# Two units' MLP by blocks as the weights come, not three; the third and fourth unit's by block products

## The chip, the cores and the metric

The kernel runs on 1 core of one Trainium2 chip. The metric is the device time of one execution in microseconds (us). The core has TensorE (PE; PEld is its weight loads), VectorE (DVE), ScalarE (ACT), GpSimd (POOL) and SyncE (SP), which issues nearly all DMAs here. Each engine works through its own list of instructions in order and waits on semaphores for the others.

## The reference

An outer-product recurrence (HGRN2) for 4 batches, 8 heads, 768 tokens and head dimension 48, and then an MLP without bias over its output, all in f32:

```python
f = 1.0 / (1.0 + np.exp(-f_logit))
for t in range(S):
    state = f[:, :, t, :, None] * state + np.einsum('bhd,bhe->bhde', k[:, :, t], v[:, :, t])
    y[:, :, t] = np.einsum('bhd,bhde->bhe', q[:, :, t], state)
x = np.ascontiguousarray(y.transpose(0, 2, 1, 3)).reshape(B * S, H * D)   # 3072 x 384
h = x @ w_in                                                              # 384 x 2048
g = h * (1.0 / (1.0 + np.exp(-1.702 * h)))
out = g @ w_out                                                           # 2048 x 384
```

## The kernel before, in words

**Units.** The 3072 tokens are cut into 12 units of 256 (`U`), three to a batch. `attention(n)` returns the parts of one unit's recurrence: loads of f, q, k into `raw`, transposes into `F` and `X`, level after level of products of scores (`sc`), the states (`st`) and the output `y`, which ScalarE copies into `yT` and DMAs bring into `xT`, transposed as the MLP wants it. VectorE multiplies X by decays (L519, L523), moves scores into `A` (L466, L485) and computes the states (L667, L668).

**Weights.** w_in and w_out come in 16 pairs of column or row blocks. `fetch_weights` loads a pair into one of three `bits` buffers, and `begin_pair` and `convert` turn it into usable f32: one ScalarE activation (L228) and four VectorE instructions (L230 to L233), the last of which writes `w_in` or `w_out`. The 16 pairs make four blocks of the hidden dimension, each with two pairs of w_in and then two of w_out; pairs 12 and 13 are the fourth block of w_in, 14 and 15 that of w_out. The temporaries are `a` and `s`; `s` has one buffer.

**MLP.** There are three forms. *By blocks* (`mlp_block`, with `mlp_h`, L1100, and `mlp_o`, L1114): per block of four tiles of the hidden dimension, 12 matmuls of 256 columns make h, and 8 of 384 columns make a partial sum of the output, which ScalarE copies to `sum` for the first block and VectorE adds to it for the later ones (L1164, L1166). *h by block products* (`mlp_h20`, L1006): a 4 x 3 by 3 x 2 block product with 20 multiplications of sums of blocks in place of 24, so 80 matmuls of 128 columns in place of 48 of 256. It needs sums of the blocks of x (`E`, twelve additions on GpSimd, `sums_of_x`, L968) and sums of blocks of w_in: nine new tiles `N_c1` to `N_p16` (`sums_of_w`; L930 and L928, mostly on GpSimd), and nine that overwrite w_in itself (`sums_in_place`, four on GpSimd, five on VectorE), after which no plain h is possible. ScalarE and VectorE combine the products into `g` (L1013 to L1036). *o by seven products* (`mlp_o7`, L869): a 2 x 2 block product with seven multiplications, 56 matmuls of 192 columns in place of 32 of 384. It needs sums of quarters of w_out (`T`, `sums_of_b`, L783) and of g (`S`, `sums_of_a`, L804 to L813), on VectorE.

**Who uses which.** Before the change units 0, 1 and 2 go by blocks for both h and o, since the weights are still coming; unit 3 (`mlp_unit`) has plain h and o by seven products, and from unit 4 on both are block products. `N_FILL` is 3.

**Order.** The order of TensorE and GpSimd is written out. `merge(n, fill, columns, share, pieces, ...)` emits the parts of attention unit n in turn, the beginnings of unit n + 1 among them, and after each part so many items of `fill` (the list of MLP matmuls with their columns) as make up its share of `columns`; `pieces` says how many pairs are converted within it and `chores` lists sums to be done in between. Up to `fill_order.close()`, after the merge of unit 3, the order of the other engines is also that of emission; later it is planned by the framework. `LAG`, `UNIT`, `H20` are numbers of columns.

**Banks.** PSUM tiles of the MLP take four banks in turn (`bank`, tags mm0 to mm3); h20 also uses the tags `y` and `sc` of the attention (its lanes 4 and 5 are the tile `h_y`). A product that takes a bank waits for whoever last reads it.

Of the kernel before, what the change touches and what calls it, by code (L numbers as in the profile page):

```python
# [23 lines left out]
def kernel(  # L24
# [33 lines left out]
    nc = tc.nc  # L58
    B, H, S, D = q.shape
    DM = H * D  # L60
# [4 lines left out]
    U = 256  # L65
# [7 lines left out]
    NK = DM // P  # L73
    NFF = DFF // P
    FG = 4
    PAIRS_AHEAD = 3
    N_FILL = 3
    HALF = U // 2
    SLOT = NP * HALF
    NA = NP * U  # L80
# [20 lines left out]
    turns = count()  # L101
# [72 lines left out]
    NGR = NFF // FG  # L174
# [144 lines left out]
    def attention(n):  # L319
# [265 lines left out]
        def turn_k(a0):  # L585
            if a0 == 0:
                new_kn()
            if n < N_FILL + 1:
                pt = bank([P, 2, 2, P], f"tkn_{n}_{a0}")
            else:  # L590
                pt = ps.tile([P, 2, 2, P], F32, tag="sc", name=f"tkn_{n}_{a0}")
            for a in range(2):
                for f in range(2):
                    x = (a0 + a) * HALF
                    nc.tensor.transpose(pt[:, a, f, :], slot((KR, KF)[f])[:, x:x + HALF], ident)
            nc.scalar.copy(t["kn"][:, a0:a0 + 2], pt)
# [75 lines left out]
        def _():  # L672
# [4 lines left out]
            for cs in ((1, 0), (2, 3)):  # L677
                for a in range(NP):
                    for c in cs:
                        g, f = CHUNK[c]  # L680
# [5 lines left out]
                        for h in range(2):  # L686
                            state = t["before"][c][rows(h), a] if w > 1 else t["ahead"][rows(h), NC - 1, a]
                            x = a * HALF + g * HS
# [29 lines left out]
            xTs[n] = xT  # L718
            if n == 0:
                fetch_weights()  # L720
            if n > N_FILL:
                sums_of_x(n)

        def whole(py):
# [402 lines left out]
    def mlp_unit(n, fill):  # L1127
        g, before = {}, []

        def last_token():  # L1130
            po = ps.tile([P, DM], F32, tag="sc", name="o_last")
            nc.tensor.matmul(po[:1], lhsT=ones, rhs=g["last"][:, 0], start=True, stop=True)
            nc.scalar.copy(g["last"][:1, 0], po[:1])
            nc.sync.dma_start(out=out[NALL * U - 1:, :], in_=g["last"][:1, 0])
        o = mlp_o7(n, g)
        if width(n) > U:
            o.insert(6 * HF, (DM, last_token, 0))
        if width(n) > U:
            before = fill[-2 * HF:]
            del fill[-2 * HF:]  # L1140
        if n > N_FILL:
            return mlp_h20(n, g, before) + o
        by_block = {}

        def end():

            g[0], g[1] = (by_block["tile", i] for i in range(2))
            sums_of_a(n, g)
            sums_in_place(nc.gpsimd)
            lanes["o"] = [next(turns) % 4 for _ in range(4)]  # L1150
        return mlp_h(n, range(NFF), by_block) + [(0, end, 0)] + o[:HF] + [(0, lambda: sums_in_place(nc.vector), 0)] + o[HF:]

    sums = {}

# [16 lines left out]
    def mlp_blocks(*blocks):  # L1171

        hs, os = zip(*(mlp_block(n, r) for n, r in blocks))
        return sum(hs, []) + sum(os, [])
# [44 lines left out]
    def merge(n, fill, columns, share, pieces=0, hold=0, by=1.0, chores=[], per=3, deal=()):  # L1219
# [10 lines left out]
        for kind, fn in parts:  # L1230
            ready = state["done"]
            while kind in ("S", "S1") and any(in_y.get(m) for m in range(n)):
                w, emit, _ = fill.pop(0)
                emit()
                done += w
            fn()
            at += share(kind)
            at_ops += converting.get(kind, 0)
            most = pieces * NOP // 2
            n_ops = min(int(most * at_ops / (by * total_ops)), most) - ops  # L1240
            if deal:
                n_ops, deal = deal[0], deal[1:]
            ops += n_ops
            first, n_columns = done, max(0, columns * (at - held) / (total - held) - done)

            def some(end):
                nonlocal done
                while fill and done < end and fill[0][2] <= ready:
                    w, emit, _ = fill.pop(0)
                    emit()  # L1250
                    done += w
            jobs = [convert] * n_ops + chores[:per]
            del chores[:per]
            for i, job in enumerate(jobs):
                some(first + n_columns * i / len(jobs))
                job()
            some(first + n_columns)
# [12 lines left out]
    def opening():  # L1270
# [44 lines left out]
        for _ in range(NOP):  # L1315
            convert()

    fill = []
    opening()
    fill += mlp_blocks((0, 0)) + mlp_blocks((0, 1))  # L1320
    merge(1, fill, UNIT // 2 - LAG // 2 - 3 * DM, steady, 13, hold=1)
    fill += mlp_blocks((1, 0), (1, 1)) + mlp_blocks((0, 2), (1, 2))
    merge(2, fill, UNIT + 3 * DM, steady, 12)
    fill += mlp_blocks((2, 0), (2, 1)) + mlp_blocks((2, 2), (0, 3)) + mlp_blocks((1, 3), (2, 3))
    w_sums = [*sums_of_w(("c3", "p15", "c2", "p6"))]
    merge(3, fill, 3 * UNIT // 2 - LAG // 2, steady, 5, by=0.7, chores=w_sums, per=1)
    fill_order.close()
    for n in range(N_FILL, NALL):
        fill += mlp_unit(n, fill)
    with nc.allow_non_contiguous_dma("one token"):  # L1330
        for h in range(2):
            nc.sync.dma_start(out=q_end[h * HS:h * HS + D], in_=q[B - 1, h::2, S - 1, :].rearrange("a d -> d a"))
    assert not w_sums
    of_b = [*sums_of_b()]
    for x in sums_of_w(("c1", "c4", "p12", "p4", "p16")):
        w_sums += of_b[:1] + [x]
        del of_b[:1]
    w_sums += of_b
    for n in range(4, NALL):
        merge(n, fill, (H20 if n > N_FILL + 1 else NFF * NK * U) + 7 * HF * HC, late, chores=w_sums if n == 4 else [])  # L1340
    for _, emit, _ in fill:
        emit()

# [28 lines left out]
```

## Time and profile before

| | |
|---|---|
| median of 3 runs | 598.24 us (596.16 to 599.87) |
| span of the profiled execution, first to last instruction | 594.5 us |
| TensorE busy, matmuls | 574.9 us, 97% |
| VectorE busy | 429.5 us, 72% |
| ScalarE busy | 291.9 us, 49% |
| GpSimd busy | 138.4 us, 23% |
| plain h, L1100 | 384 passes |
| plain o, L1114 | 192 passes |
| conversions of pairs end (last write of w_out) | 171.7 us from the start |
| first block product of o (unit 3) | 224.0 us |
| first block product of h (unit 4) | 248.4 us |

The span is that of one profiled execution; the runs' time also holds what lies around the first and last instruction, so 594.5 stands beside 598.24, a difference of 3.7 us. A matmul in f32 shows as two passes in the trace, and counts of passes are twice those of the program. In the timeline's rows the columns are start, duration, engine, line, operation, tiles, shape and count, and in brackets the idle time before and who ended it; in the windows' rows they are busy time of PE, PEld, DVE, ACT and POOL, each with its number of instructions, then the granted TensorE clock, the share of DMA and GB/s.

### The profile page before, as it was taken

The page shows a single profiled execution, that of the slowest core. Times are in us where ns is not written, and L with a number is a line of the kernel's source. Part 1 is how long each engine was busy: PE and PEld are TensorE (multiplying, and loading weights), DVE is VectorE, ACT ScalarE, POOL GpSimd, SP SyncE. Part 2 cuts the span into 40 slices and gives each one's busy share as a digit, 9 for nine tenths or more (in the row PEclk, how much of TensorE's full clock was granted, in tenths as well). Part 3 has the DMA queues.
Part 4 walks back from the last instruction along what each step waited for, and adds up shares of the span by engine and source line. Part 5 has one row for each costly group of instructions (what it writes and reads, how often), then busy time and mean ns, then how long its engine had stood idle before and what let it go on. Part 6 is the DMA issues. An engine that isn't in the chain of part 4 may idle for free.

```text
span 594.5 us, 18457 instructions
## 1 busy us (share of the span) xinstructions
PE 574.9 (97%) x7814; PEld 513.6 (86%) x7814; DVE 429.5 (72%) x696; ACT 291.9 (49%) x613; POOL 138.4 (23%) x214
## 2 busy tenths in 40 slices
PE   6879899999999999999999999999999999999997
PEld 6756776867768789999999999999999999999897
DVE  2898987964866858789778778786887786462284
ACT  4746643453334353474474474573663564452440
POOL 4031200230027216610610700800700602203000
PEclk9979999999999999999999999999999999999999
DMA  7947859840243552353552343553361211001000
GB/s 181 215 124 179 193 145 225 217 100 1 52 106 66 145 130 65 80 139 77 127 146 51 84 113 91 130 134 60 88 168 44 63 38 29 28 3 27 28 1 27
DMA packets 82834, 58.29 MB, mean 98 GB/s; under 512 B 33153, under 2 KB 74785, under 8 KB 82753
## 3 DMA queue, kind: packets, MB, share of 16 engines
q1 hardware_dynamic: 82416, 56.73, 38.9%
q8 instruction: 61, 1.00, 0.7%
q10 hardware_dynamic: 337, 0.39, 0.3%
q14 instruction: 20, 0.16, 0.1%
HBM read 43.98 MB, written 8.39 MB: 88 GB/s over the span
## 4 chain that ended last, share of the span: by engine, by line
PE 87%; DVE 7%; ACT 3%; issue 1%; DMA 1%; POOL 1%; SPq 0%; DVEq 0%; ACTq 0%
PE h L1006 17%; PE h L1100 13%; PE o_Y L869 11%; PE o L1114 10%; PE o_Z L869 8%; PE h_y L1006 6%; PE sc L425 6%; PE o_X L869 4%; PE o_W L869 4%; PE y L689 2%; PE t L357 2%; PE y L534 2%; PE sc L643 1%; DVE X L519 1%; ACT yT L703 1%
## 5 line engine op out<-in xcount | busy, mean ns | idle before, releaser
L1100 PE MATMUL h<-xT,w_in 128*128 128x256 f32 x384 | 89.6, 388 | 1.4 <-DMA xT<-yT 1.4
L523 DVE TENSOR_TENSOR X<-X,tot 128x1024 f32<-128x1024 f32 x45 | 57.0, 1266 | 39.8 <-PE sc L425 33.2
L1100 PEld LDWEIGHTS h<-xT,w_in 128*128 128x128 f32 x384 | 72.8, 193 | 13.8 <-DMA xT<-yT 2.4
L494 ACT COPY Kc<-X 128x512 f32<-128x512 f32 x72 | 48.4, 672 | 65.7 <-DVE X L523 51.5
L1114 PE MATMUL o<-w_out,g 128*128 128x384 f32 x192 | 65.5, 491 | 0.4 <-DVE w_out L233 0.4
L968 POOL TENSOR_TENSOR E<-xT 128x128 f32<-128x128 f32 (+1 forms) x32 | 17.9, 571 | 204.0 <-DMA xT<-yT 112.0
L1114 PEld LDWEIGHTS o<-w_out,g 128*128 128x128 f32 x192 | 35.4, 190 | 22.8 <-DVE w_out L233 1.0
L1006 PE MATMUL h<-E,w_in 128*128 128x128 f32 (+1 forms) x420 | 53.4, 275 | 0.0
L869 PE MATMUL o_Y<-T,S 128*128 128x192 f32 x288 | 50.6, 329 | 0.0
L1006 PEld LDWEIGHTS h<-E,w_in 128*128 128x128 f32 x420 | 50.1, 192 | 0.0
L1036 ACT ACTIVATE g<-g 128x512 f32<-128x512 f32 (+1 forms) x63 | 35.6, 584 | 26.0 <-DVE g L1034 25.3
L1104 ACT ACTIVATE g<-h 128x256 f32<-128x256 f32 x64 | 23.8, 382 | 49.0 <-PE h L1100 48.6
L869 PEld LDWEIGHTS o_Y<-T,S 128*128 128x128 f32 x288 | 46.8, 190 | 0.5
L1034 DVE TENSOR_TENSOR g<-g,h 128x512 f32<-128x512 f32 (+1 forms) x52 | 31.8, 632 | 14.3 <-PE h L1006 13.3
L485 DVE COPY_PREDICATED A<-masks,sc 128x256 f32<-128x256 uint32 (+1 forms) x98 | 42.0, 506 | 0.1
L703 ACT COPY yT<-y 48x256 f32<-48x256 f32 x88 | 32.2, 366 | 18.3 <-PE y L689 17.2
L372 POOL TENSOR_SCALAR F<-F 128x1024 f32<-128x1024 f32 x10 | 17.2, 1716 | 95.9 <-ACT F L375 84.3
L345 DVE STREAM_TRANSPOSE X<-raw 128x512 f32<-128x512 f32 x36 | 38.1, 1105 | 0.1
L425 PEld LDWEIGHTS sc<-X,Kc 48*64 48x64 f32 x1440 | 26.2, 136 | 11.1 <-ACT Kc L494 4.8
L425 PE MATMUL sc<-X,Kc 48*64 48x64 f32 x1440 | 31.0, 222 | 4.8 <-ACT Kc L494 1.9
L1034 DVE TENSOR_TENSOR g<-g,h_y 128x512 f32<-128x512 f32 (+1 forms) x26 | 16.5, 634 | 22.3 <-PE h_y L1006 21.4
L1025 ACT ACTIVATE g<-h 128x512 f32<-128x512 f32 (+1 forms) x46 | 26.1, 576 | 10.8 <-PE h L1006 10.6
(162 smaller groups left out, 1156.2 us busy)
## 6 DMA issues: line engine op xcount, KB each, us to landing
bits<-in_moe_w_out_dram SPq DMA_DIRECT2D x8, 768.0 KB, 7.2
raw<-in_f_logit_dram SPq DMA_DIRECT2D x48, 96.0 KB, 3.5
raw<-in_k_dram SPq DMA_DIRECT2D x48, 96.0 KB, 3.0
bits<-in_moe_w_in_dram SPq DMA_DIRECT2D x8, 576.0 KB
raw<-in_q_dram SPq DMA_DIRECT2D x44, 96.0 KB, 2.3
k_tok<-z SPq DMA_DIRECT2D x56, 64.0 KB, 1.8
kt<-k_tok SPq DMA_DIRECT2D x14, 256.0 KB, 2.8
out_dram<-osb SPq DMA_DIRECT2D x18, 192.0 KB, 2.7
```

Of the source, the lines that this page charges most:

```text
L345: nc.vector.transpose(view(out, at, [[HALF, NP], [step, R4], [R4 * step, 32]]), by_half[:, j, f].rearrange("p a (j d) -> p (a j) d", j=R4) ...
L425: nc.tensor.matmul(t["sc"][h][g * HS:(g + 1) * HS, a, s, :], lhsT=t["Kc", l][rows(h), x:x + HS], rhs=rhs(h, a, g), start=True, stop=True,)
L485: moved = nc.vector.copy_predicated(out=view(A, c * HALF + at, dims), mask=mask.bitcast(U32), data=got)
L494: nc.scalar.copy(c.rearrange("p (n two m) -> p n two m", two=2, m=m), view(X, KF * SLOT, [[2 * m, SLOT // (2 * m)], [(KR - KF) * SLOT + m, ...
L523: nc.vector.tensor_tensor(x, x, y, ALU.mult)
L703: nc.scalar.copy(view(yT[rows(h)], at, [[U, NP], [step, HS]]), py[columns(h, g), g, :, f, :])
L869: nc.tensor.matmul(t[name], lhsT=lhs(f), rhs=rhs(f), start=(new and i == 0), stop=(i == HF - 1), skip_group_check=True,)
L1006: nc.tensor.matmul(ph[:, t], lhsT=WA[a][:, f * P:(f + 1) * P], rhs=E[n][b], start=(root and t == 0), stop=not goes_on, skip_group_check=True,)
L1034: nc.vector.tensor_tensor(to, to, part, ALU.add if sign > 0 else ALU.subtract)
L1036: nc.scalar.activation(to, to, AF.Gelu_apprx_sigmoid)
L1100: nc.tensor.matmul(ph, lhsT=w_in[:, c, ff * P:(ff + 1) * P], rhs=xTs[n][:, c, :], start=(c == 0), stop=(c == NK - 1))
L1114: nc.tensor.matmul(t["po"], lhsT=g[ff // FG][:, ff % FG, tt * P:(tt + 1) * P], rhs=w_out[:, ff, :], start=(ff == ffs[0]), stop=(ff == ffs[ ...
```

## The change

`N_BLOCK` is 2: only units 0 and 1 have all four blocks of the plain form. Their fourth block comes from `last_blocks()`, which puts the sums of w_in that are still to be done, the sums of unit 2's x and the sums in place into the list behind the first o of that block. Unit 2 gets h and o by block products (`first_whole`, with the sums of w_out's quarters spread over its h), and unit 3's h becomes block products as well, since `mlp_unit` knows no plain form any more. All nine sums of w_in are chores of the merge of unit 3, two per part, and the last conversions come earlier: 13 pieces in the merge of unit 2 (12 before), 4 in that of unit 3 (5 before), spread over its first part (`by` 0.3, was 0.7). In the later merges every unit has `H20 + 7 * HF * HC` columns and no chores.

```diff
+    N_BLOCK = 2
...
-            if n < N_FILL + 1:
+            if n < N_FILL:
                 pt = bank([P, 2, 2, P], f"tkn_{n}_{a0}")
...
-            if n > N_FILL:
+            if n >= N_FILL:
                 sums_of_x(n)
...
-        if n > N_FILL:
-            return mlp_h20(n, g, before) + o
-        by_block = {}
-
-        def end():
-
-            g[0], g[1] = (by_block["tile", i] for i in range(2))
-            sums_of_a(n, g)
-            sums_in_place(nc.gpsimd)
-            lanes["o"] = [next(turns) % 4 for _ in range(4)]
-        return mlp_h(n, range(NFF), by_block) + [(0, end, 0)] + o[:HF] + [(0, lambda: sums_in_place(nc.vector), 0)] + o[HF:]
+        return mlp_h20(n, g, before) + o
...
-            jobs = [convert] * n_ops + chores[:per]
-            del chores[:per]
+            jobs = [convert] * n_ops + [lambda: chores and chores.pop(0)()] * per
...
+    def last_blocks():
+
+        hs, os = zip(*(mlp_block(n, NGR - 1) for n in range(N_BLOCK)))
+
+        def sums_of_w_left():
+            for x in w_sums:
+                x()
+            w_sums.clear()
+            sums_of_x(N_BLOCK)
+            sums_in_place(nc.gpsimd)
+            sums_in_place(nc.vector)
+            lanes["o"] = [next(turns) % 4 for _ in range(4)]
+        o = sum(os, [])
+        return sum(hs, []) + o[:1] + [(0, sums_of_w_left, 0)] + o[1:]
+
+    def first_whole(n):
+
+        h, of_b = mlp_unit(n, fill), [*sums_of_b()]
+        while of_b:
+            x = of_b.pop()
+            h.insert(2 * len(of_b) + 4, (0, x, 0))
+        return h
...
-    merge(2, fill, UNIT + 3 * DM, steady, 12)
-    fill += mlp_blocks((2, 0), (2, 1)) + mlp_blocks((2, 2), (0, 3)) + mlp_blocks((1, 3), (2, 3))
-    w_sums = [*sums_of_w(("c3", "p15", "c2", "p6"))]
-    merge(3, fill, 3 * UNIT // 2 - LAG // 2, steady, 5, by=0.7, chores=w_sums, per=1)
+    merge(2, fill, UNIT + 3 * DM, steady, 13)
+    fill += last_blocks() + first_whole(N_BLOCK)
+    w_sums = [*sums_of_w(("c3", "p15", "c2", "p6")), *sums_of_w(("c1", "c4", "p12", "p4", "p16"))]
+    merge(3, fill, 2 * UNIT + H20 + 7 * HF * HC - LAG - (3 * UNIT // 2 - LAG // 2), steady, 4, by=0.3, chores=w_sums, per=2)
...
-    assert not w_sums
-    of_b = [*sums_of_b()]
-    for x in sums_of_w(("c1", "c4", "p12", "p4", "p16")):
-        w_sums += of_b[:1] + [x]
-        del of_b[:1]
-    w_sums += of_b
     for n in range(4, NALL):
-        merge(n, fill, (H20 if n > N_FILL + 1 else NFF * NK * U) + 7 * HF * HC, late, chores=w_sums if n == 4 else [])
+        merge(n, fill, H20 + 7 * HF * HC, late)
```

## Prediction

> **What bounds the kernel now.** The page came first, parts 1 and 2. Line numbers are those of the kernel before; each `x` counts passes, two for every f32 matmul of the program.
>
> ```profile
> PE 574.9 (97%) x7814; PEld 513.6 (86%) x7814; DVE 429.5 (72%) x696; ACT 291.9 (49%) x613; POOL 138.4 (23%) x214
> PEclk9979999999999999999999999999999999999999
> ```
>
> TensorE sets the time: some 20 us idle in 594.5, nearly all in the first 70 us and the last 50. VectorE is free 28% of the span, GpSimd 77%. So less matmul work shortens the kernel wherever TensorE stays fed, and any new wait on its strictly ordered queue is paid in full. Next the TensorE timeline, for the price of each kind of pass (start, duration, engine, line):
>
> ```profile
> 142.49 7.90 PE L1114 MATMUL o<-w_out,g 128*128 128x384 f32 x24
> ...
> 205.78 18.40 PE L1100 MATMUL h<-xT,w_in 128*128 128x256 f32 x84
> 224.01 2.11 PE L869 MATMUL o_Y<-w_out,g 128*128 128x192 f32 x12
> ...
> 236.70 2.76 PE L869 MATMUL o_Y<-T,S 128*128 128x192 f32 x16
> 239.30 2.76 PE L869 MATMUL o_Z<-T,g 128*128 128x192 f32 x16
> ...
> 251.46 1.95 PE L1006 MATMUL h<-E,w_in 128*128 128x128 f32 x16
> 253.25 1.06 PE L1006 MATMUL h_y<-E,N_c 128*128 128x128 f32 x8
> ```
>
> Start to start: a plain h pass 18.23/84 = 0.217 us, a plain o pass 0.33, a pass of o7 2.60/16 = 0.163, one of h20 1.79/16 = 0.112. No idle stands between these rows. Third, the GpSimd and VectorE timelines, for the sums that h20 needs first:
>
> ```profile
> 190.23 1.27 POOL L930 TENSOR_TENSOR N_p<-w_in 128x512 f32<-128x512 f32 x1
> 191.46 2.26 POOL L930 TENSOR_TENSOR N_p<-N_p,w_in 128x512 f32<-128x512 f32 x1
> ...
> 224.26 3.19 POOL L930 TENSOR_TENSOR w_in<-w_in 128x512 f32<-128x512 f32 x2 [14.39 <-PE h L1100]
> 227.41 2.94 POOL L930 TENSOR_TENSOR w_in<-w_in,N_c 128x512 f32<-128x512 f32 x2
> ...
> 242.51 0.87 POOL L968 TENSOR_TENSOR E<-xT 128x128 f32<-128x128 f32 x2 [8.45 <-DMA xT<-yT]
> ...
> 249.05 0.87 POOL L968 TENSOR_TENSOR E<-E,xT 128x128 f32<-128x128 f32 x2
> ```
>
> ```profile
> 109.16 0.96 DVE L232 SCALAR_TENSOR_TENSOR a<-bits,a 128x768 f32<-128x768 uint32 x1
> 110.15 0.96 DVE L233 TENSOR_TENSOR w_in<-a,s 128x768 f32<-128x768 f32 x1
> ...
> 143.69 0.58 DVE L309 STREAM_SHUFFLE vt<-vr 128x384 f32<-128x384 f32 x1
> ...
> 227.49 1.74 DVE L930 TENSOR_TENSOR w_in<-N_c,w_in 128x512 f32<-128x512 f32 x1 [1.17 <-POOL w_in L930]
> ```
>
> A 128x512 sum on GpSimd takes 1.27 us, or 2.26 where VectorE works beside it; the twelve sums of x run 242.51 to 249.92, 7.4 us.
>
> **The change part by part.** *Matmul work removed.* Units 2 and 3 go from 96 plain h passes (20.8 us) to 160 of h20 (17.9): -2.9 each. Unit 2 goes from 64 plain o passes (21.1) to 112 of o7 (18.2): -2.9. That is -8.7; unit 4's h takes 18.45 us on the timeline, not 17.9, because banks change more often, so I take -7.5.
>
> *Work added elsewhere.* VectorE 686 to 711 instructions, ScalarE 621 to 628, GpSimd 219 to 243, SyncE 516 either way. In the steady unit period (y to y, 270.53 to 313.74 = 43.2 us) the same work already lies under TensorE, so from unit 3 on it costs nothing. The weight DMAs are the same; the last pair is fetched around 112 us, takes 7.2 us to land (part 6) and is used at 144. No cost. What costs is the order at the hand-over to unit 2's h20.
>
> *Pair 13 earlier.* Two more conversion instructions (0.96 each) stand ahead of unit 2's state sums on VectorE. These ended at 117.18 while TensorE began y at 116.69, so there is no slack: +1.5 us (0 to 1.9).
>
> *The last pair.* After unit 1's third block TensorE is at 132.3. Then: unit 0's fourth block h (24 passes, 5.2), scores (1.09), unit 1's h (5.2), scores (1.09), so 144.9 for the first o, which needs pairs 14 and 15 of w_out. On VectorE pair 15's four instructions (3.1 us) stand behind the shuffle that ends at 144.27: ready at 147.5, against 146.2 when it is wanted. +1.25 (0 to 2). TensorE has done all 32 o passes at 156.9.
>
> *The sums, the main cost.* h20's first product of unit 2 takes the bank that unit 1's o filled; the order of instructions shows it waiting for that o's addition on VectorE (third of four sums). This addition stands behind VectorE's half of `sums_in_place`, whose product p9 overwrites w_in rows that GpSimd's p3 still reads; and p3 stands behind `sums_of_x(2)` and `N_p16`, which takes the conversion's "s" buffer and so starts only after pair 15, at 147.6. From there: N_p16 and N_p12 2 x 1.27; N_p15 waits for N_p4 (VectorE, 150.5), 1.27 to 2.24; N_p16 1.27; twelve sums of x 5.9 (sum of their 0.46 without VectorE beside them) to 7.4; k and p3 2.6 to 3.2: p3 ends at 162.2 to 165.3. Then p9, p5, p11 (2.1 to 3.5) and three sums at 0.55: the bank is free at 166 to 170.5. Behind p9 also queue the first sums of b and the transposes of unit 4's F, for which ScalarE waits. I take 168, nearer the uncontended rows because VectorE idles meanwhile. TensorE has been idle since 156.9: +11.1 (9 to 13.6).
>
> *The clock after it.* Slow matmuls follow idle stretches in the windows of the start:
>
> ```profile
> 36.00:40.00 4.00, 2.47 (x35) 1.59 (x35) 3.93 (x7) 1.32 (x3) 0.00 (x0) 0.50 0.42 76
> 40.00:44.00 4.00, 4.00 (x18) 3.08 (x20) 3.83 (x6) 0.78 (x3) 0.00 (x0) 0.67 0.94 290
> ```
>
> The granted clock (third from the right) was 0.50 and 0.67, and 12 h passes from 38.40 to 43.60 took 5.2 us for 2.6. I take +2 after the long idle (0 to 2.6).
> The Trainium skill (TensorE: Matmul & The Clock Gate, Part 1) says that TensorE falls to half rate after an idle window of about 3.4 us and needs about as long busy to recover; by it an estimate is 3.4/2 = 1.7 us, against 0 if the clock held.
>
> *The second wait.* Unit 3's y follows h20 in TensorE's order, and its bank is h_y's, freed by the eighth g sum (L1034). From 168 VectorE has, in order: a sum, two of `sums_of_b`, four transposes, one of b: 7.3 us. The first g sum waits for h20's ninth product, 9 x 0.89 + 2 for the clock = 10. From there: eight g sums (0.65 each, 5.2), five more of b (0.95 each, 4.75), two transposes (2.0), ScalarE's two copies of X (1.3) and the product of X after them (1.2), and about 2 more where g sums wait for TensorE or for ScalarE's gelus: some 27 us after the bank came free. TensorE alone needs 18.45 + 1.0 of transposes = 19.4. So +7.4, the clock's 2 within it (3 to 10). In the steady period the eighth ends at 268.9, ahead of y at 270.53: the cover there is a VectorE that has no sums of b and no backlog.
>
> Sum: -7.5 + 1.5 + 1.25 + 11.1 + 7.4, less 0.3 for an idle at 234 that goes, = +13.4. The span of 594.5 becomes 608; the 3.7 us between the span and the median of 598.24 are kept: 611.6.
>
> **Rivals.** *Hidden chain, faster.* The o passes of the last block would cover the sums if GpSimd started about 9 us sooner: were pair 15 converted right behind pair 14 (by 138), p3 would end near 154, the bank come free as TensorE arrives, and 598.2 - 7.5 + 1.5 = 592 results. GpSimd's 77% idle speaks for it; against it, on VectorE pair 15 stands behind products of X that wait for scores ending at 138.6. It decides from the moment the bank comes free by about 158. *First wait only.* VectorE catches up before y: 598.2 - 7.5 + 2.75 + 9 = 602.5. For it: VectorE's g sums wait for TensorE anyway; against: 7 us of sums of b and transposes stand between them. *Contention throughout.* Every GpSimd sum at its dear row (170.5), second wait 10, and unit 3's states late by 2 more: 598.2 - 7 + 3 + 13.6 + 10 + 2 = 620. For it: rows of 2.26; against: VectorE waits during that chain.
>
> **How the numbers follow.** Forecast 0.65 (606 to 617), first wait only 0.16, contention 0.11, hidden 0.08. The time is the forecast's, 611.5. The low end, 602, takes in the first-wait case, the high end, 619, most of contention. About 1% (6 us) is what a measurement here can tell from no change; beyond it faster takes most of the hidden case, 0.06, within it lies most of first-wait, 0.13, slower is 0.81.
>
> **What the profile after would show.** Right: an idle of 9 to 14 us ahead of the first h20 product near 157, ended by VectorE's o sum; a VectorE gap ended by GpSimd's w_in; a clock below 1 in that slice; a wait before unit 3's y; 192 plain h passes for 384; periods of 43.2 from unit 3 on. Wrong: GpSimd done by 158, or h20 starting before 160.

## The result, and the profile after

The changed kernel takes 617.38 us (median of four runs, 616.90 to 622.77) beside 598.75 us for the kernel before: a ratio of 1.034 (95% interval 1.029 to 1.039). It is slower, as forecast. The 611.5 us of the forecast fall 6 us short: 617.38 lies just above the 606 to 617 of its main case and inside its outer range of 602 to 619. The profiled execution took 617.48 us, with a span of 615.7 us (594.5 before). Line numbers of the changed kernel are those of the kernel before plus one from line 78 on, up to L1140; the o sums are L1157 here (L1166 before). An experiment's edit shifts them by up to 15 lines more.

From the page of the changed kernel: busy times of the engines, and the TensorE clock in 40 slices of 15.4 us.

```profile
PE 572.9 (93%) x7990; PEld 523.0 (85%) x7990; DVE 449.5 (73%) x721; ACT 300.4 (49%) x620; POOL 151.6 (25%) x238
PEclk9979999999979899999999999999999999999999
```

TensorE's share falls from 97 to 93%: fewer columns, more waiting. The clock dips in the twelfth and the fourteenth slice, where it was full before. TensorE's timeline gives every wait between 100 and 550 us; the four short ones behind that, 2.15 us together, are in the kernel before too (start, duration, engine, line, count, and in brackets the idle time ahead and what ended it):

```profile
108.05 1.56 PE L1101 MATMUL h<-xT,w_in 128*128 128x256 f32 x6 [0.55 <-DVE sum L1157]
110.84 0.65 PE L596 MATMUL tkn<-ident,X 128*128 128x128 f32 x4 [1.22 <-DVE sum L1157]
...
137.63 3.11 PE L1101 MATMUL h<-xT,w_in 128*128 128x256 f32 x12 [1.24 <-DVE sum L1157]
141.13 1.56 PE L1101 MATMUL h<-xT,w_in 128*128 128x256 f32 x6 [0.39 <-DVE sum L1157]
...
152.56 9.30 PE L1115 MATMUL o<-w_out,g 128*128 128x384 f32 x28 [0.77 <-DVE w_out L234]
173.34 3.67 PE L1007 MATMUL h<-E,N_c 128*128 128x128 f32 x16 [11.48 <-DVE sum L1157]
...
200.13 1.96 PE L535 MATMUL y<-A,vt 64*48 64x64 f32 x64 [6.17 <-DVE g L1035]
...
220.05 0.69 PE L426 MATMUL sc<-Qc,Kc 48*64 48x64 f32 x32 [0.73 <-DVE A L486]
```

Five small waits on VectorE's o sums and on the last pair, then the long one ahead of unit 2's h20, then the one ahead of unit 3's y, then a new one at unit 4's scores. After that (unit 4's y at 248.51, unit 5's at 291.71) the period is 43.2 us, as before.

The chain behind the long wait, from GpSimd's timeline and then VectorE's:

```profile
152.59 2.19 POOL L931 TENSOR_TENSOR N_p<-w_in 128x512 f32<-128x512 f32 x1 [12.79 <-DVE w_out L234]
...
159.75 0.86 POOL L969 TENSOR_TENSOR E<-xT 128x128 f32<-128x128 f32 x2
...
165.17 2.60 POOL L931 TENSOR_TENSOR w_in<-w_in 128x512 f32<-128x512 f32 x2
```

```profile
167.80 1.73 DVE L931 TENSOR_TENSOR w_in<-N_c,w_in 128x512 f32<-128x512 f32 x1 [9.13 <-POOL w_in L931]
169.46 2.35 DVE L931 TENSOR_TENSOR w_in<-w_in,N_c 128x512 f32<-128x512 f32 x2
171.73 1.93 DVE L1157 TENSOR_TENSOR sum<-sum,o 128x384 f32<-128x384 f32 x4
```

GpSimd stands 12.8 us, until pair 15 has left the buffer that N_p16 takes, four sums and E follow, k and p3 end at 167.8, VectorE has waited 9.1 us for them, and only behind p9, p5 and p11 come the o sums that free the bank. This is the chain of the forecast, link by link.

The clock after it (windows of 2 us: length, then PE, PEld, DVE, ACT and POOL busy, the granted clock, DMA share, GB/s):

```profile
164.00:166.00 2.00, 0.00 (x0) 0.00 (x0) 0.00 (x0) 0.00 (x0) 1.92 (x4) 1.00 0.00 0
...
168.00:170.00 2.00, 0.00 (x0) 0.00 (x0) 2.00 (x2) 0.00 (x0) 2.00 (x2) 0.50 0.00 0
...
174.00:176.00 2.00, 2.00 (x11) 2.00 (x11) 2.00 (x3) 0.57 (x1) 0.00 (x0) 0.50 0.83 291
...
178.00:180.00 2.00, 2.00 (x21) 2.00 (x20) 2.00 (x3) 1.36 (x3) 0.00 (x0) 1.00 0.65 162
```

And VectorE's row ahead of unit 3's y, from the sixth g sum on:

```profile
191.31 0.68 DVE L1035 TENSOR_TENSOR g<-g,h 128x512 f32<-128x512 f32 x1
191.91 2.04 DVE L346 STREAM_TRANSPOSE X<-raw 128x512 f32<-128x512 f32 x2
195.46 1.23 DVE L524 TENSOR_TENSOR X<-X,F 128x1024 f32<-128x1024 f32 x1 [1.51 <-ACT Qc L501]
197.92 0.69 DVE L1035 TENSOR_TENSOR g<-g 128x512 f32<-128x512 f32 x1 [1.23 <-ACT g L1026]
198.53 0.95 DVE L784 TENSOR_TENSOR T<-T,w_out 128x768 f32<-128x768 f32 x1
199.40 0.68 DVE L1035 TENSOR_TENSOR g<-g,h_y 128x512 f32<-128x512 f32 x1
```

Between the sixth g sum and the seventh lie 5.9 us of unit 4's `begin_k`: two transposes, a wait for ScalarE's Kc and Qc, a product of X, a wait for ScalarE's next Kc and the gelu queued behind it. TensorE had ended h20 at 194.0.

**The ledger.** The spans differ by 21.2 us. Of these 1.1 are there at 52 us already, where both programs are the same (TensorE's first o pass of that place stands at 51.44 and 52.57): variation of the start. From there to unit 2's y (L535, 114.40 against 110.64) 2.65 are lost; the three waits at 137 to 153 us are 2.4; the first wait 11.5; the clock in h20 1.65 (the run that keeps TensorE warm, below: h20's first to last group 17.92 us, here 19.57); the second wait 6.2; and after it 0.7 at the scores and 1.8 of clock (y to o_W 6.45 us here, 4.67 in the run whose y did not wait). That is 28.0, so the matmul work that went is 28.0 - 21.2 = 6.8 us: a remainder, not a measurement of its own. The medians differ by 18.6 us, not 21.2. In every recorded run the time is 2.1 to 2.2 us above the span for the kernel before and 1.7 to 1.8 us for the others, so the profiled execution of the kernel before (594.5) was some 1.6 us faster than its median one; the 1.1 us at the start are probably part of that.

### The profile page after: what moved, and what is told of

Read it like the earlier page. It is cut to its first block, busy times and chain, and to the rows that moved or that the text cites. A ratio compares the mean times of both kernels' runs of the same rounds, so it can differ in the third digit from the quotient of the medians.

```text
span 615.7 us, 18902 instructions
## 1 busy us (share of the span) xinstructions
PE 572.9 (93%) x7990; PEld 523.0 (85%) x7990; DVE 449.5 (73%) x721; ACT 300.4 (49%) x620; POOL 151.6 (25%) x238
## 4 chain that ended last, share of the span: by engine, by line
PE 73%; DVE 14%; ACT 3%; issue 3%; DMA 3%; POOL 2%; SPq 2%; DVEq 0%; POOLq 0%; ACTq 0%
PE h L1007 21%; PE o_Y L870 12%; PE o_Z L870 8%; PE h_y L1007 7%; PE sc L426 5%; PE o_W L870 4%; PE o_X L870 4%; PE t L358 2%; PE y L535 2%; PE o L1115 2%; DVE X L524 2%; PE y L690 2%; PE sc L644 1%; DVE a L233 1%; PE h L1101 1%
## 5 line engine op out<-in xcount | busy, mean ns | idle before, releaser
L1007 PE MATMUL h<-E,w_in 128*128 128x128 f32 (+1 forms) x532 | 67.6, 275 | 0.0
L1007 PEld LDWEIGHTS h<-E,w_in 128*128 128x128 f32 x532 | 63.5, 192 | 0.0
L1037 ACT ACTIVATE g<-g 128x512 f32<-128x512 f32 (+1 forms) x77 | 44.3, 592 | 33.6 <-DVE g L1035 32.7
L1101 PE MATMUL h<-xT,w_in 128*128 128x256 f32 x192 | 47.5, 397 | 4.6 <-DMA xT<-yT 2.3
L1035 DVE TENSOR_TENSOR g<-g,h 128x512 f32<-128x512 f32 (+1 forms) x64 | 39.6, 641 | 15.8 <-PE h L1007 13.5
L1101 PEld LDWEIGHTS h<-xT,w_in 128*128 128x128 f32 x192 | 36.3, 196 | 12.1 <-DVE sum L1157 3.8
L1115 PE MATMUL o<-w_out,g 128*128 128x384 f32 x128 | 44.0, 493 | 1.2 <-DVE w_out L234 1.2
L1007 PE MATMUL h<-E,N_c 128*128 128x128 f32 (+1 forms) x236 | 34.0, 289 | 11.5 <-DVE sum L1157 11.5
L704 ACT COPY yT<-y 48x256 f32<-48x256 f32 x88 | 32.2, 366 | 19.6 <-PE y L690 18.6
L1007 PEld LDWEIGHTS h<-E,N_c 128*128 128x128 f32 x236 | 30.9, 201 | 12.8 <-issue 12.1
L1026 ACT ACTIVATE g<-h 128x512 f32<-128x512 f32 (+1 forms) x58 | 33.3, 582 | 13.6 <-PE h L1007 13.4
L1115 PEld LDWEIGHTS o<-w_out,g 128*128 128x128 f32 x128 | 23.5, 190 | 16.6 <-DVE w_out L234 1.9
L426 PEld LDWEIGHTS sc<-X,Kc 48*64 48x64 f32 x1440 | 26.2, 136 | 11.1 <-ACT Kc L495 4.9
```

The source lines that it names most:

```text
L426: nc.tensor.matmul(t["sc"][h][g * HS:(g + 1) * HS, a, s, :], lhsT=t["Kc", l][rows(h), x:x + HS], rhs=rhs(h, a, g), start=True, stop=True,)
L1007: nc.tensor.matmul(ph[:, t], lhsT=WA[a][:, f * P:(f + 1) * P], rhs=E[n][b], start=(root and t == 0), stop=not goes_on, skip_group_check=True,)
L1026: nc.scalar.activation(to, ph, AF.Copy, scale=float(sign))
L1035: nc.vector.tensor_tensor(to, to, part, ALU.add if sign > 0 else ALU.subtract)
L1037: nc.scalar.activation(to, to, AF.Gelu_apprx_sigmoid)
L1101: nc.tensor.matmul(ph, lhsT=w_in[:, c, ff * P:(ff + 1) * P], rhs=xTs[n][:, c, :], start=(c == 0), stop=(c == NK - 1))
```

## The experiments

Each kernel is the changed kernel with one edit, or with the edits named. A kernel's runs scatter by 1 to 7 us, so beside the ratio the table gives what one trace resolves better: the time from the start of unit 2's y to that of unit 4's, which leaves the start-up out. Four kernels with the same code from unit 2's y to the first product of h20 take 58.94 to 59.02 us there (changed, c_warm, e_late_k, q_late_k_noT), and from unit 4's y to TensorE's last instruction all thirteen take 364.1 to 364.5 us. Where an edit moves unit 2's y itself (d_pieces12, o_pool_conv), the stretch doesn't hold the whole effect. The kernel before took 597.81 to 598.92 us beside them.

| kernel | median us | ratio to before (95%) | unit 2's y to unit 4's y, us |
|---|---|---|---|
| changed | 617.38 | 1.034 (1.029-1.039) | 134.1 |
| x_early | 614.08 | 1.029 (1.026-1.031) | 130.8 |
| a_vec_after_o | 615.05 | 1.029 (1.027-1.031) | 131.8 |
| c_warm | 617.06 | 1.033 (1.031-1.036) | 132.4 |
| d_pieces12 | 617.60 | 1.034 (1.032-1.037) | 137.0 |
| e_late_k | 617.21 | 1.031 (1.028-1.034) | 133.5 |
| b_gap | 622.36 | 1.039 (1.036-1.041) | 138.5 |
| f3_own_p15 | 611.82 | 1.021 (1.018-1.024) | 126.3 |
| l_early_late_k | 610.15 | 1.019 (1.016-1.022) | 126.8 |
| n_conv_less | 614.84 | 1.027 (1.024-1.030) | 131.6 |
| q_late_k_noT | 615.23 | 1.028 (1.024-1.032) | 133.3 |
| m_all | 607.65 | 1.015 (1.009-1.021) | 122.8 |
| o_pool_conv | 608.35 | 1.016 (1.013-1.020) | 126.5 |

(The kernel before takes 115.4 us over that stretch, with the matmul work spread otherwise.)

**The first wait: whose order?**

```
 def sums_of_w_left():                        # x_early
-    for x in w_sums:
+    for x in w_sums[:-4]:
         x()
-    w_sums.clear()
     sums_of_x(N_BLOCK)
+    for x in w_sums[-4:]:
+        x()
+    w_sums.clear()
```

> Edit: GpSimd makes unit 2's data sums (E) while it would stand in its 12.8 us wait for w_out's pair 14, and not behind p16, p12, p15 and p16. Theory (GpSimd's row of sums sets the first wait: p3 holds VectorE's p9, and p9 holds the o sums that free the bank): E's 5.4 us leave the row, p3 ends at about 162.4 us, not 167.8, TensorE's wait ahead of h20 shrinks from 11.5 to about 6 us, y after h20 starts at about 195 us, not 200, and the kernel takes about 612 us (5 less than the changed kernel's 617.4). Rival (the second wait is due by something that doesn't hang on the first, such as unit 4's transposes and ScalarE): the first wait shrinks, the second grows by as much, and the time stays within 1 us of 617.

```profile
145.15 0.87 POOL L969 TENSOR_TENSOR E<-xT 128x128 f32<-128x128 f32 x2 [2.98 <-PE h L1101]
...
151.62 0.46 POOL L969 TENSOR_TENSOR E<-xT 128x128 f32<-128x128 f32 x1 [2.72 <-PE h L1101]
```

```profile
171.57 3.75 PE L1007 MATMUL h<-E,N_c 128*128 128x128 f32 x16 [6.74 <-DVE sum L1157]
```

GpSimd's timeline first, TensorE's second. The first wait falls to 6.7 us as the theory said, and the second keeps its 6.17, so the rival is out. The gain is 3.3 us, not 5: E's buffers are still read by plain h passes, and E stops twice for them; and the low clock behind the wait lasts longer, so that h20 to y takes 27.6 us, for 26.8. (The expectation names pair 14; by the trace GpSimd waits for pair 15, whose last step ends at 152.5 us in the changed kernel.)

```
-            sums_in_place(nc.vector)         # a_vec_after_o
...
-        return ... + o[:1] + [(0, sums_of_w_left, 0)] + o[1:]
+        return ... + o[:1] + [(0, sums_of_w_left, 0)] + o[1:] + [(0, lambda: sums_in_place(nc.vector), 0)]
```

> Edit: VectorE's five sums in place (p7, p19, p9, p5, p11) stand behind its eight additions of o in its order, not ahead of them. Theory (it is the order on VectorE, an o addition behind p9, that keeps the bank from h20): the first wait for an o addition goes; h20's first products start by about 165 us, not 173.3, and stop for p9 or for E for some 2 to 4 us in all; the granted clock stays near 1.0. The second wait (y for the eighth g sum) grows, since VectorE's rows are only some 3 to 5 us earlier: y at about 195 us, not 200.1, and a time of about 612 us. Rival (GpSimd's sums alone set it): h20 waits for p3 or p9 as long as it waited for the bank, and the time moves by less than 2 us.

```profile
178.65 0.68 DVE L1035 TENSOR_TENSOR g<-g,h_y 128x512 f32<-128x512 f32 x1
```

```profile
161.81 1.95 PE L1007 MATMUL h<-E,N_c 128*128 128x128 f32 x16
...
169.85 2.02 PE L1007 MATMUL h<-E,w_in 128*128 128x128 f32 x16 [2.52 <-DVE w_in L931]
...
179.42 2.05 PE L1007 MATMUL h_y<-xT,w_in 128*128 128x128 f32 x8 [5.33 <-issue]
...
197.78 1.96 PE L535 MATMUL y<-A,vt 64*48 64x64 f32 x64 [5.94 <-DVE g L1035]
```

One row of VectorE, then TensorE's timeline: the first wait is gone and h20 begins at 161.8 with no idle ahead. So the o sums' place behind p9 is what holds the bank. But h20 then stops for 2.5 us (p9) and for 5.3 us. The profile names nobody who ends the second stop. The last thing to end ahead of it is VectorE's first g sum (at 179.33), which reads h_y and stands behind sums of b and four transposes without a gap; ScalarE's copy of h, behind unit 4's F activation, had ended at 177.3. The 11.5 us come back as 7.9 and a clock of 0.50 until 185.3 us, and 2.4 us are left of the gain; I had expected 5.

```
+        for _ in range(20):                  # c_warm, behind the last o
+            nc.tensor.matmul(pt, lhsT=ident, rhs=masks..., start=True, stop=True)
```

> Edit: 20 matmuls of 320 columns whose result nobody reads (some 10.7 us at the full clock) stand behind the last o pass, so that TensorE is busy during the first wait. The work added is left out of the result. Theory (the clock that falls to 0.5 after an idle stretch of 11.5 us costs about 2 us): the granted clock is 1.0 from 165 to 180 us, the first 16 passes of h20 take 1.8 us, not 3.7, y starts at about 198 us, and the kernel takes about 615.5 us, 2 less. Rival (the second wait is due by VectorE, and takes up what the clock gives): h20 ends 2 us earlier, the wait of y for the eighth g sum is 8 us, not 6.2, and the time is that of the changed kernel within 0.5 us.

```profile
174.64 2.02 PE L1007 MATMUL h<-E,N_c 128*128 128x128 f32 x16 [0.75 <-DVE sum L1157]
...
199.78 1.96 PE L535 MATMUL y<-A,vt 64*48 64x64 f32 x64 [6.16 <-DVE g L1035]
```

Sixteen passes take 2.02 us for 3.67, the clock stays at 1.00 until 196 us, the wait ahead of y stays (so the rival is out), and the stretch is 1.7 us shorter: the price of the first clock drop, close to the 2 forecast. The median moves by 0.3 us only, which the scatter doesn't tell from 1.7.

**GpSimd's row without its two waits.** `sums_of_w` gives N_p16 a tile of its own, and p15 is made without VectorE's p4:

```
-            if name == "p16":                # f3_own_p15
-                WA[name] = wp.tile([P, 2 * DM], F32, tag="s", ...)[:, :FG * P]
-            else:
+            if True:
                 WA[name] = const.tile(...)
...
-            ("p15", "p15", "", "p4"),
+            ("p15", "p15", "+", "c1"), ("p15", "p15", "+", "a30"),
```

> Edit: N_p16 has a buffer of its own instead of the conversion's s, and GpSimd makes p15 from c1 and a row of w_in instead of from VectorE's p4 (one more GpSimd sum), so that GpSimd's row waits neither for pair 15's conversion nor for VectorE. Theory (GpSimd's sums start only with pair 15's conversion, and that places p3): the four or five w sums are done by about 147 us, not 159.8; E runs in 146 to 155 us, in part behind the plain h passes up to 149 us that still read its buffers; p3 ends at about 159 us, not 169; the bank is free at 163 to 164 us, the first wait falls from 11.5 to about 2 us, the clock stays at 1.0, and with a second wait of 6 us still there the kernel takes about 607.5 us, 10 less. Rival (VectorE and ScalarE then have unit 4's F, transposes and sums of b in their way, as they stopped h20 for 5.3 us when only VectorE's order was changed): h20 starts as early, but takes 4 to 6 us longer, and 612 to 614 us result.

```profile
149.72 0.69 PE L426 MATMUL sc<-Qc,Kc 48*64 48x64 f32 x32 [1.75 <-DVE A L486]
...
150.81 12.47 PE L1113 MATMUL o<-w_out,g 128*128 128x384 f32 x32
165.96 2.02 PE L1005 MATMUL h<-E,N_c 128*128 128x128 f32 x16 [2.68 <-DVE sum L1155]
...
191.10 1.96 PE L535 MATMUL y<-A,vt 64*48 64x64 f32 x64 [6.17 <-DVE g L1033]
```

The first wait is 2.7 us, for 11.5, and behind it the clock is 1.00: the largest single gain (7.8 us in the trace, 5.6 in the medians). Of the 8.8 us less of waiting, 6.2 are h20 beginning earlier after unit 2's y, and 2.6 are TensorE arriving later. That GpSimd's sums start with pair 15 is thus the main cause. The second wait stays at 6.17. It also costs something: scores at 149.7 us wait 1.75 us for VectorE, whose two products of X take 2.0 and 2.2 us beside GpSimd's sums (1.23 in the changed kernel), and behind that short stop the granted clock is 0.50 from 151.0 to 154.4 us, so that the 32 o passes take 12.47 us (10.59 in m_all at the full clock).

```
+            for x in sums_of_b():            # b_gap
+                x()
             sums_in_place(nc.vector)
...
-        h, of_b = mlp_unit(n, fill), [*sums_of_b()]
+        h, of_b = mlp_unit(n, fill), []
```

> Edit: all eight sums of b stand on VectorE ahead of its sums in place, in the 9 us in which it waits for p3, not spread over h20. Theory (the second wait is a chain through h20's late products, the transposes and ScalarE): the sums of b among the last g sums cost it 2 x 0.95, so y starts about 2 us earlier after h20's start; but GpSimd works beside a busy VectorE (E and p3 dearer), so that the bank comes free 1 to 2 us later: 616 to 617.5 us. Rival (VectorE's amount of work sets the second wait): 7.6 us leave its row, the wait goes, y starts at about 195 us, 612 us.

```profile
157.87 3.96 DVE L784 TENSOR_TENSOR T<-w_out 128x768 f32<-128x768 f32 x2
161.75 3.15 DVE L784 TENSOR_TENSOR T<-w_out,T 128x768 f32<-128x768 f32 x2
```

```profile
162.91 2.30 POOL L969 TENSOR_TENSOR E<-xT 128x128 f32<-128x128 f32 x2
```

```profile
181.34 3.75 PE L1007 MATMUL h<-E,N_c 128*128 128x128 f32 x16 [16.86 <-DVE sum L1157]
...
207.01 1.96 PE L535 MATMUL y<-A,vt 64*48 64x64 f32 x64 [4.63 <-DVE g L1035]
```

VectorE, GpSimd, TensorE. The gap is not free: two sums of b take 3.96 us (1.81 in the changed kernel), two of E 2.30 (0.86), the first wait grows to 16.9, and the kernel loses 4 to 5 us where 616 to 617.5 us had been expected. With 4.8 us of sums of b taken from between the g sums, y follows h20's start by 25.7 us, for 26.8: VectorE's amount of work alone is not what sets the second wait.

**The second wait.** Unit 4's `begin_k` is emitted when all of h20 has been:

```
-    parts += [("B", begin_k), ...            # e_late_k
+    parts += [("BK" if n == N_FILL else "B", begin_k), ...
-            while kind in ("S", "S1") and any(in_y...
+            while kind in ("S", "S1", "BK") and any(in_y...
```

> Edit: unit 4's begin_k (two X transposes, the copies Kc and Qc, a product of X) is put behind the last product of unit 2's h20, not among its last products. In the four kernels run so far y stands 5.9 to 6.2 us after h20 wherever h20 starts, so the second wait seems to be a chain behind h20's late products and not a backlog of VectorE. Theory (that chain: the sixth g sum, the transposes 2.0, Kc and Qc 1.5, the product of X 1.2, Kc 0.6, only then ScalarE's next gelu, the seventh and eighth g sums): with the attention part behind it the wait falls from 6.2 to about 2 us, y starts at about 196 us, not 200.1, and the kernel takes about 613.4 us, 4 less. Rival (VectorE's amount of work from 173 us on): the wait falls by what is moved off VectorE alone, 3.2 us at most, and the five sums of b still hold the last g sum. Second rival: the chain moved behind y comes late for unit 4's first scores (220 us), which wait as much longer: no gain.

```profile
196.21 1.11 PE L535 MATMUL y<-A,vt 64*48 64x64 f32 x64 [0.34 <-DVE g L1035]
...
217.93 1.13 PE L426 MATMUL sc<-Qc,Kc 48*64 48x64 f32 x32 [3.19 <-DVE A L486]
...
219.85 4.79 PE L870 MATMUL o_Y<-T,S 128*128 128x192 f32 x16
```

The wait goes from 6.2 to 0.3 us, so `begin_k` is its cause. But the second rival holds too: unit 4's scores now wait 3.2 us, S 0.9, and the clock falls after that (o_Y 4.79 us for 2.87). Of 5.1 us 0.6 are left.

```
 def sums_of_b():                             # q_late_k_noT: e_late_k and this
+    T[1], T[2], T[3] = (quarter(w_out, *at) for at in ((0, 1), (1, 1), (0, 0)))
+    T[4] = lambda f: quarter(w_out, 1, 0)[:, f]
+    return []
```

> Edit: unit 4's begin_k behind unit 2's h20, as before, and the eight sums of b are left out (their tiles stand for rows of w_out, so that o is wrong in value). With the first alone y came 5 us earlier, but unit 4's scores then waited 3.2 us and S 0.9 us, at a lower clock, and all but nothing was left. Theory (behind the chain VectorE's row is the next bound, some 30 us without a gap, and the sums of b are 7.6 us of it): y stays at about 195 us, the waits at 209 and 218 us and the low clock after them go, unit 4's h20 begins at about 220 us, not 226, and the kernel takes about 611 us. Rival (the row there is set by the g sums, S, the transposes and the scores in a chain, and VectorE only looks full): as with begin_k moved alone, 617 us.

```profile
216.83 1.13 PE L426 MATMUL sc<-Qc,Kc 48*64 48x64 f32 x32 [3.21 <-DVE A L486]
```

My theory fails: without any sum of b the scores wait the same 3.21 us. What lies on VectorE from the last g sum (196.1) to the mask that frees the scores' bank (216.7) has no sum of b in it: transposes and product of `begin_k` 4.8 us with the 1.5 us in which VectorE waits for ScalarE's Kc and Qc, the state sums 2.7, S and the sums of g about 7, transposes and products of X 5, masks 2. That wait is the only gap of the row behind the last g sum, so `begin_k` costs its 5 us on one side of y or on the other.

```
l_early_late_k = f3_own_p15 and e_late_k
```

> Edit: both: N_p16's own buffer with p15 without VectorE's p4, and unit 4's begin_k behind unit 2's h20. Theory (two separate waits, each with its own chain): the gains add, 10 and 4, to about 603.5 us; what is left above the kernel before (some 5 us) is what stands before the last o passes. Rival (one resource, VectorE's row from 163 us on, sets both): the sum is no more than the better of the two alone.

```profile
188.74 1.11 PE L535 MATMUL y<-A,vt 64*48 64x64 f32 x64 [0.34 <-DVE g L1033]
...
210.47 1.13 PE L426 MATMUL sc<-Qc,Kc 48*64 48x64 f32 x32 [3.21 <-DVE A L486]
```

The gains don't add: 126.8 us over the stretch against 126.3 with the first edit alone. The time is the rival's, but that doesn't show one resource behind both waits: moving `begin_k` brought only 0.6 us by itself, for the reason just seen.

**Ahead of the last o passes.**

```
-    merge(2, fill, UNIT + 3 * DM, steady, 13)        # d_pieces12
+    merge(2, fill, UNIT + 3 * DM, steady, 12)
-    merge(3, fill, ..., steady, 4, by=0.3, ...)
+    merge(3, fill, ..., steady, 5, by=0.3, ...)
```

> Edit: 12 pieces, not 13, in the second part of the plan (as before the change), and 5, not 4, in the third, so that pair 13 is converted where it was before. Theory (the thirteenth piece puts every conversion of pairs 11 to 13 earlier, ScalarE's activation of pair 11 waits 7.65 us for its DMA, and VectorE's o sums stand behind it): TensorE's waits at 108 to 111 us go, it reaches y at 111.8 us, not 114.4, and stands some 2.5 to 3 us earlier at 124 us; the last pair comes up to 1 us later, so that the kernel takes about 614.5 to 615.5 us. Rival (TensorE waits there anyway, the last pair sets the end of the o passes): the passes of o end at 161.9 us as in the changed kernel, and the time is the same within 0.7 us.

```profile
147.18 5.49 PE L1101 MATMUL h<-xT,w_in 128*128 128x256 f32 x12 [3.85 <-ACT g L1105]
```

```profile
142.89 0.62 ACT L495 COPY Kc<-X 128x512 f32<-128x512 f32 x1 [6.38 <-DVE X L524]
```

The waits at 108 to 111 us go and y stands at 111.83, but the conversions now lie at 133 to 142 us: VectorE's product of X comes late, ScalarE's Kc stands 6.4 us for it with the gelus queued behind, and TensorE waits 3.85 us at 147, with the clock at 0.50 behind that until 153.3 us. No gain: the time is the rival's, though not its sign, for the o passes end at 164.6 us, not 161.9, and the first wait is 9.1 us for it. (The stretch of 137.0 us begins at an earlier y: unit 4's y stands at 248.9, for 248.5.)

```
+        if m >= len(pairs) - 2:              # n_conv_less
+            todo[-4:-2] = [lambda: None] * 2
```

> Edit: the conversions of w_out's pairs 14 and 15 (the last two) take two VectorE instructions, not four; the second and third (0.56 and 0.96 us) are left out, so that those rows of w_out have wrong values. Theory (VectorE's row between 100 and 152 us, into which the change pulls the last pairs' conversions, sets the waits of 4.2 us that TensorE has there, since the o sums that free its banks stand among the conversions): 3.0 us go from that row, TensorE's waits at 138, 141 and 153 us (2.4 in all) go or nearly so, the last o pass ends at about 159.5 us, not 161.9, GpSimd's sums begin as much earlier, and the kernel takes about 614.5 us. Rival (TensorE's own order of passes and the scores set it, as when 12 pieces were put for 13): the waits move elsewhere, and the time is within 1 us of 617.

```profile
171.35 3.58 PE L1009 MATMUL h<-E,N_c 128*128 128x128 f32 x16 [10.95 <-DVE sum L1159]
```

With 3.0 us of conversion gone from VectorE, two of the three waits at 138 to 153 us go, the o passes end 1.9 us earlier after unit 2's y, and the stretch is 2.5 us shorter (614.84 us, 614.5 expected). Moving conversions moves the wait; removing them removes most of it (1.25 us at 138 stay). VectorE's row between 100 and 152 us holds up what stands ahead of the last o passes.

**All together, and the best version.**

```
m_all = f3_own_p15, e_late_k, n_conv_less and no sums of b
```

> Edit: all that helped, at once: N_p16's own buffer and p15 without p4, begin_k behind h20, the two cut conversions, no sums of b (the last two leave work out). Theory (four places, each with a price of its own: waits ahead of the last o passes 4, first wait with its clock 11 to 13, second wait with its clock 8 to 9, all of it VectorE's row or GpSimd's sums ahead of it): the waits add up, and with most of them gone the time is about 600 to 602 us, near the kernel before, with 2 to 3 us of TensorE waits left at the first product of h20 and at the scores. Rival (something else than these four is dear, for instance h20 and o7 themselves in units 2 and 3): 606 us or more in spite of the waits being gone.

```profile
166.03 2.44 PE L992 MATMUL h<-E,N_c 128*128 128x128 f32 x16 [3.51 <-DVE sum L1142]
...
207.95 0.76 PE L428 MATMUL sc<-Qc,Kc 48*64 48x64 f32 x32 [3.19 <-DVE A L488]
```

607.65, not 600 to 602. The waits had not gone as far as I thought: 12.4 us of idle are left between 100 and 540 us (0.9, 1.2, 1.3, 1.8, 3.5, 0.5, 3.2), and the clock takes about 1.6 in h20 and 1.6 after the scores. The ledger still closes: 12.4 + 3.2 - 6.8 = 8.8 us above the kernel before, and 607.65 - 598.92 = 8.7 were measured. That it closes to 0.1 us is luck, since m_all's four runs lie between 603.56 and 610.63; a hidden price of more than a few us in h20 and o7 themselves is ruled out, a smaller one is not.

```
-            lambda: ve.tensor_tensor(dst, a, s, ALU.add),    # o_pool_conv: l_early_late_k and this
+            lambda: (nc.gpsimd if m in (9, 10, 11, 12, 13) else ve).tensor_tensor(dst, a, s, ALU.add),
```

> Edit: N_p16's own buffer, p15 without p4, begin_k behind h20 (610.2 us as run), and the last step of the conversion (a plus s, 0.96 us) of pairs 9 to 13 on GpSimd, which stands idle from 77 to 111 us. Nothing is left out. Theory (VectorE's row sets the waits at 108 to 111 us): 4.8 us leave it, those waits (1.8 us) and a part of the later ones go, about 608 us. Rival (the two engines hold each other up, as the sums of b did beside E, where a 128x768 sum took 1.98 for 0.95 us): each GpSimd step takes 2 us or more and holds VectorE's products up by as much, and pair 13 comes later: 610 to 612 us.

```profile
104.69 1.83 POOL L234 TENSOR_TENSOR w_out<-a,s 128x768 f32<-128x768 f32 x1 [7.66 <-DVE a L233]
```

608.35 us, as the theory had it, though the 1.8 us gained over l_early_late_k lie within the scatter of both (the traces show 0.4 over the stretch and 0.5 ahead of unit 2's y): each such step takes GpSimd 1.8 us, the one shown beside VectorE's transposes of F, which keep their pace, and of the waits at 108 to 111 us 0.9 is left of 1.8. It is the best version found, 9 us below the change and still 1.6% above the kernel before, which none of them beats.

## Where the forecast was right, and which steps failed

Term by term, against the ledger:

| step of the forecast | forecast us | measured us |
|---|---|---|
| matmul work removed | -7.5, and -0.3 for an idle | -6.8 |
| pair 13 earlier | 1.5 | 2.65 |
| the last pair | 1.25 | 0.77, and 1.63 in two waits that no term holds |
| the sums, first wait | 11.1 | 11.5 |
| second wait, with the clock | 7.4 | 6.2 + 1.65 |
| after the second wait | 0 | 2.5 |
| the start of the execution | 0 | 1.1 |

*Right.* Direction, both waits, what ends the first, and their sizes. That the sums bound the first wait is shown by f3_own_p15 (11.5 to 2.7) and x_early (to 6.7), the order on VectorE by a_vec_after_o (to 0), the clock by c_warm. The forecast had the bank free at 168; it came free at 173.3, of which 1.1 is the start and the rest the o passes and pair 15 being later; the chain itself kept its length. (The twelve sums of x took 5.4 us; the 5.9 of the forecast is a slip, as 12 x 0.46 is 5.5.) The *contention throughout* rival gave 620, near the truth, but for other reasons: the first wait was 11.5 and not 13.6, and the sums ran at 1.3 to 1.7 us but for the first (2.19), not all at 2.26. The *hidden chain* rival, 592, is not what its nearest test gives: f3_own_p15 hides all but 2.7 us of the chain and 5.6 to 7.8 us come of it, since the second wait and what follows don't hang on the first. *First wait only* (602.5) fell with the 6.2 us ahead of y.

Together the differences make the 7.7 us between the forecast span of 608 and 615.7. In the medians the forecast is 5.8 us off (611.6 for 617.38), because the 3.7 us that it kept between span and time are 1.8 in the changed kernel: the profiled execution of the kernel before was a fast one.

*Failed: the size of "Pair 13 earlier" and "The last pair"*, 2.75 for 5.05. I priced the two steps by the instructions put ahead of one reader each. The change pulls the last pairs' conversions into a VectorE row that is busy for 40.3 of the 52 us from 100 to 152 us (34.5 before), and there o sums that free TensorE's banks, products of X and ScalarE's copies all stand behind them. The waits at 137.6 and 141.1 us, on o sums among pair 14's instructions, are in no term of the forecast. n_conv_less shows the row to be the cause of one of them and of the last pair's wait, d_pieces12 that another place for pair 13 only moves the wait. The 2.65 itself scatters: it is 1.3 to 4.3 us in the ten other kernels that leave pair 13 as it is, 2.3 in the middle; without the thirteenth piece (d_pieces12) nothing of it is left.

*Failed: the cause in "The second wait", and its end at y.* The forecast added up a VectorE row of 27 us and put the wait down to the sums of b and a backlog in it; then the steady period was to begin at once. The row did take 26.8 us, but that is partly luck: b_gap takes 4.8 us of sums of b out of it, and y comes 1.1 us earlier. The runs put `begin_k` in their place, which the forecast had in its sum as 4.5 us among others: e_late_k moves it and the wait goes. What the forecast put at nothing behind y measured 2.5 us: the idle of 6.2 us costs clock a second time, 1.8 us, which I had counted only after the long one, and 0.7 more is a VectorE row that is late for unit 4's scores.

*The rest* is 1.1 us at the start, where no code differs (TensorE's first o pass of that place stands at 51.0 to 54.6 us in the thirteen traces), and 1 us less removed from TensorE than forecast. As that 6.8 is a remainder, these runs don't tell where the 1 us went.

## What to carry to other kernels

When a change lets one engine's work start earlier, price what is pulled ahead against the whole row of each in-order engine there, not against the next reader: here conversions, o sums and copies shared one VectorE queue, and a wait taken from one place came back at the next. A gap in an engine's row is not free for work that slows down whoever causes the gap: in b_gap it cost 4 to 5 us. And a stop of TensorE can be paid twice: in these runs every one of 3.09 us or more was followed by a spell at half clock, and one of 1.75 us as well.

## What the hardware showed that I had not expected

*How a stop costs clock.* Read in windows of 0.25 us, the granted clock is 1.00 or 0.50 but for the windows in which it changes. The changed kernel and its twelve variants have 26 spells at 0.50 between 100 and 262 us, and each lasts 3.41 us (5 of them), 6.83 (15), 10.24 (3), 13.65 (2) or 17.07 us (1): whole multiples of 3.41. In each trace with more than one, their beginnings too lie a whole number of such steps apart (in the changed kernel 166.55 and 197.27 us, 9 steps). So a stop is paid by steps of a beat that doesn't begin with it. The kernel before has no such spell there. They set in 2.0 to 5.1 us after TensorE stopped, some when it was at work again: after 3.09 us of idle (l_early_late_k) the clock was 1.00 in the idle stretch itself and 0.73, 0.50 and 0.92 in the three windows of 2 us after work had begun, so that 16 passes of h20 took 2.74 us for 2.02. The length of the stop doesn't decide alone: all 25 stops of 3.09 us or more were followed by a spell, those of 2.51 (a_vec_after_o) and 2.68 us (f3_own_p15) were not, and of four stops of 1.75 us in the same place one was (f3_own_p15) and three were not (l_early_late_k, m_all, o_pool_conv). The Trainium skill (TensorE: Matmul & The Clock Gate, Part 1) gives an idle window and a recovery of about 3.4 us each. The step of the spells agrees with that figure; as a limit on the length of a stop it doesn't hold here, and the full clock came back 3.3 to 6.6 us after work had begun again.

*VectorE and GpSimd side by side.* In b_gap a 128x768 sum of two SBUF operands took 1.98 us on VectorE, for 0.9 alone, while GpSimd's 128x128 sums took 1.15 for 0.43. Some 7.6 us of work on VectorE and 6 on GpSimd, at their durations without the other, took 11.4 us side by side, little less than one after the other. The Trainium skill (SBUF — State Buffer, Who interferes with whom) says that a VectorE instruction with two SBUF inputs contends with a GpSimd instruction that reads SBUF; the run agrees, and adds the price. Transposes took their usual 1.0 us each beside GpSimd's 128x768 sum (o_pool_conv, two in 2.06 us).
